# Twelve chunks untiled, unit 4 by crossbar, unit 0's v through TensorE, unit 7's decays by small transfers: a re-planned attention and FFN kernel

## The chip, the cores and the metric

The kernel runs on one core of a Trainium2 chip. A core has TensorE (PE, matrix products into PSUM), VectorE (DVE), ScalarE (ACT), GpSimd (POOL) and SyncE (SP), which share the on-chip memory SBUF and sixteen DMA engines. In this kernel SP issues the transfers of the hardware queue (loads, stores, and transpositions through the DMA crossbar); POOL issues the weights on the software queue, which turn from float32 into bf16 on the way. The metric is the device time of one execution in microseconds (us). Before the change it is 196.26 us, the median of three runs (196.06 to 196.44).

## What is computed

```python
f = 1.0 / (1.0 + np.exp(-f_logit))                  # (4, 8, 768, 48)
state = np.zeros((B, H, D, D))
for t in range(S):
    state = f[:, :, t, :, None] * state + np.einsum('bhd,bhe->bhde', k[:, :, t], v[:, :, t])
    y[:, :, t] = np.einsum('bhd,bhde->bhe', q[:, :, t], state)
x = y.transpose(0, 2, 1, 3).reshape(B * S, H * D)   # 3072 tokens, 384 wide
gate = np.maximum(x @ w_gate, 0.0)                  # 1536 wide
out = (gate * (x @ w_val)) @ w_out
```

A gated linear attention (4 batches, 8 heads, 768 tokens, head size 48) feeds an FFN with two input matrices and one output matrix.

## The kernel before

**Units and chunks.** A chunk is 128 tokens of one batch, 24 in all. A unit is two chunks that follow each other, numbered y = 0 and 1; unit u holds chunks w = 2u and 2u + 1, and the twelve units go through the batches in turn (`seq`), so that unit u + 4 takes up the state that unit u left. Four chunks, two units, are a group of 512 tokens for the FFN; group g needs units 2g and 2g + 1. A load brings two neighbouring tokens to each partition, so even and odd tokens are apart (index i).

**A unit** (`unit`, L603). ScalarE takes exp and log of the forget logits (L620, L622). TensorE forms cumulative sums (`cum`, L629 and L630; where `even` is DVE, VectorE derives one of the two, L633), ScalarE their exponentials (L641, L644, L651; `qps` says whether q's stay in PSUM), and VectorE or POOL multiplies them into q and k, the "hats". Then there are two ways. In the units of `pe_hats` a hat is made whole (L663), and TensorE transposes it (L703), after which a copy brings it to SBUF as `qkT` (`tk`, `tq`). In the other units the hats are made in halves of 64 rows (L669) and SP sends them through the crossbar (L725). `q_lined` lists units whose q lies in order of tokens. v is put in order by copies of 64 rows: four into `vpad`, and in units of `pe_hats` two more into `vrest`, each on an engine that a dictionary names (`v00` to `v11`, `r0`, `r1`). Scores are matmuls on 48 rows, two at a time in different rows of TensorE (L739); a mask follows, on VectorE (L752) or by a copy on ScalarE and a product on POOL (L747, L749; `m00` to `m11`). `total` (L759, L763) with an exp (L768) gives the decays, `state` (L777 untiled, L787 in two row tiles for `pe_hats`) the new part of the state, which L589, L594 and L597 put together on VectorE and POOL.

**The output of a chunk** (`out_of`, L799) has two forms. Chunks in `pe_x` take `intra` (L819): 28 matmuls, 16 where there is no state yet, in four column tiles of 32, whose result is transposed already and is copied to `xT`. The others take `natural` (L826, L830): twelve untiled matmuls, a copy to `xn`, and a crossbar transposition by SP into `xT` (L848). Their rows come out with even and odd tokens apart, so their output is stored in two halves.

**The FFN.** `ffn_hidden` (L854) is for each of twelve j three gate and three val matmuls of 512 columns (L866), ScalarE's relu (L872) and VectorE's product (L878). In group 0 the first five j are done in halves of 256 columns, two chunks at a time. `ffn_out` (L883) is twelve matmuls of 384 columns for each chunk (L894), in steps of three.

**The order.** Every instruction is added to a plan with a duration, a latency, a priority (small is early) and what it reads and writes. `Plan.schedule` then simulates the engines and the two DMA rings and picks, again and again, the instruction that can start first; among equals, the one of smaller priority. Each engine executes its own list in that order, waiting on semaphores. FFN pieces form one chain with a priority of P + 60. `pace` names an FFN piece that has to start before a unit's cumulative sum may. `slack` adds 1 us to the planned end of a unit's transfers if they start after EASY = 34. While the first 24 us are planned to leave TensorE idle, it is given filler matmuls (L950, L958). `first` writes the order of the first loads; "wg2@f2" is slice 2 of w_gate, issued when f of unit 2 has landed. A load waits for the fifth load ahead of it.

```python
key = (at, op.prio, op.idx)
if u in pe_hats or (n == "q" and u not in q_lined):
if w in pe_x:
```

Of the kernel before, what the change touches and what calls it, by code (L numbers as in the profile page):

```python
# [13 lines left out]
class Op:  # L14
# [4 lines left out]
                 "after", "follows", "flow", "goal", "floor", "ring", "descs", "deps0", "crosses", "slack", "tiles", "port", "early", "held")  # L19

    def __init__(self, eng, emit, reads, writes, occ, lat, prio, opens=(), after=(), follows=()):
# [14 lines left out]
        self.port = False  # L36
        self.held = False
# [14 lines left out]
class Rings:  # L52
# [27 lines left out]
    def worked(self, t):  # L80
        work = t - self.now
        for p in self.PAUSES[self.passed:]:
            if p >= t:
                break
            work -= max(0.0, min(t, p + self.PAUSE) - max(self.now, p))
        return work

    def later(self, work):
        t = self.now
        for p in self.PAUSES[self.passed:]:  # L90
            if t + work <= p:
                break
            work -= max(0.0, p - t)
            t = max(t, p + self.PAUSE)
        return t + work

    def next(self):
        found = None
        for r, q in self.queue.items():
            if q:  # L100
                t = self.later(self.left[r] / self.speed(r))
# [6 lines left out]
    def step(self, t, ring):  # L108
        speeds = {r: self.speed(r) for r in self.RATE}
        for r, q in self.queue.items():  # L110
            if q:
                self.left[r] -= self.worked(t) * speeds[r]
# [17 lines left out]
class Plan:  # L130
# [3 lines left out]
    EASY = 26.0  # L134
    hot_until = 0.0
# [43 lines left out]

    def schedule(self, banks):  # L180
# [9 lines left out]
        free = dict(self.free0)  # L190
        waiting = {e: [] for e in self.ENGINES}
# [34 lines left out]
        while True:  # L226
            pick = None
            for e in self.ENGINES:
                for op in waiting[e]:
# [13 lines left out]
                    key = (at, op.prio, op.idx)  # L243
# [14 lines left out]
            (at, _, _), op, slot = pick  # L258
            e = op.eng
            waiting[e].remove(op)  # L260
# [92 lines left out]
def bass_hgrn2_outer__then__ffn_reglu_kernel(  # L353
# [23 lines left out]
    wsteps = 4  # L377
    WJ = NJ // wsteps
    first = 'f0 v0 f1 k0 q0 f2 wg2@f2 wg0@f2 wv0@f0 wv1@v0 k1 wg1@k1 q1 wv2@q1 v1 k2@wv0 q2 wg3@q2 wv3@v0 wo1@f0 wo0@f1 wo2@f0 wo3@f0 f3@wg2 q3@wv0 k3@wg1 v2@wo1 v3@wv0'.split()
    seq = [(0, 0), (1, 0), (2, 0), (3, 0), (0, 1), (1, 1), (2, 1), (3, 1), (0, 2), (1, 2), (2, 2), (3, 2)]  # L380
    pe_hats = {0, 1, 2, 3, 4, 5}
    pe_x = {0, 1, 2, 3, 4, 5, 6, 7, 9, 10, 11, 12, 13, 21, 22, 23}
    q_lined = {0, 1, 4, 7, 8, 9, 10}
# [20 lines left out]
    vrest = [sb(f"vrest{i}", [128, HD], BF16) for i in range(NV // 2)]  # L404
    st = [[sb(f"st{b}_{i}", [128, SW], BF16) for i in range(2)] for b in range(B)]
# [12 lines left out]
    gT = [sb(f"gT{i}", [128, NJ, GT], BF16) for i in range(NG)]  # L418
    NR = 4
# [14 lines left out]
    pl = Plan({'bc': 3, 'tp': 2, 's': 4, 'y': 1, 'kv': 2, 'f': 4})  # L434
    pl.EASY = 34
# [61 lines left out]
    for name, t, cols, value, prio in (("halves", halves, 4, 1.0, -27), ("other", other, 64, 1.0, -26), ("away", away, 16, 16.0, -26)):  # L497
# [8 lines left out]
        ["ident"], ["ident"], occ=0.25, prio=-28)  # L506
    fill("DVE", "zeros", zeros[:], 0.0, 256, -30)
# [29 lines left out]
    def load(n, u, after=()):  # L537
# [4 lines left out]
        behind = list(after) + (sent[-5:][:1] if len(sent) >= 5 else [])  # L542
        op = chain("load", "SP", lambda: sy.dma_start(dst, src), [], [f"{n}{u % NL}"], occ=0.65, lat=1.3, prio=u * 20 - 40, after=behind)
        dma(op, f"{n}{u % NL}", 1.27, 1, 1024)
# [5 lines left out]
    def load_w(nm, s, after):  # L550
        if nm == "wo":
            src = bass.AP(tensor=w_out.tensor, offset=s * WJ * 128 * DM,
                          ap=[[DM, 128], [128 * DM, WJ], [1, DM]])
            dst = wo[:, s * WJ:(s + 1) * WJ, :]
        else:
            src = bass.AP(tensor=wsrc[nm].tensor, offset=s * WJ * 128,
                          ap=[[DFF, 128], [128 * DFF, NK], [1, WJ * 128]])
            dst = (wg if nm == "wg" else wv)[:, :, s * WJ * 128:(s + 1) * WJ * 128]
        op = chain("load_w", "POOL", lambda: gp.dma_start(dst, src), [], [f"{nm}{s}"], occ=0.79, lat=2.3,
                   prio=-10 if s == 0 else 30, after=after)  # L560
        dma(op, f"{nm}{s}", 6.0 / wsteps, ring="sw")
        return op

    done = {}

    def begin(items):
        for item in items:
            item, _, behind = item.partition("@")
            need = [done[x] for x in behind.split("&")] if behind else []
# [3 lines left out]
    t4 = lambda t: t[:, 0:HD].rearrange("p (n j e) -> p n j e", n=NP, j=2)  # L573
    QROW = NQ * 4 * NP * C

# [475 lines left out]
```

## Time and profile before

| | us |
|---|---|
| median of three runs | 196.26 |
| the profiled execution, its own time | 196.28 |
| its span, first to last instruction | 194.5 |
| TensorE busy | 187.0 |
| VectorE busy | 131.1 |
| ScalarE busy | 123.2 |
| POOL busy | 75.2 |
| first FFN matmul starts | 20.38 |
| last FFN matmul group starts (60 of L894) | 184.18 |

By stretches of ten us, busy time:

| stretch | TensorE | VectorE | ScalarE | POOL |
|---|---|---|---|---|
| 0 to 10 | 8.63 | 5.10 | 6.94 | 3.81 |
| 10 to 20 | 8.73 | 8.99 | 8.22 | 7.21 |
| 20 to 30 | 9.53 | 7.65 | 7.33 | 5.29 |
| 60 to 70 | 9.79 | 9.08 | 9.87 | 6.45 |
| 110 to 120 | 9.35 | 7.96 | 5.01 | 5.61 |
| 160 to 170 | 10.00 | 4.48 | 2.98 | 0.00 |

In the profile, L866 is line 866 of the kernel. A row of the order in time gives start, duration, engine, line, operation, what is written and read, the tiling, the shape and how many instructions of that kind follow each other; in brackets stands the idle time ahead of it and what ended it. Matmuls are pipelined: a row's duration holds the time that the last one takes to leave the array, so the next row starts before it ends. What a piece costs is read from the starts. "PEld" is the loading of weights into the array, SPq and POOLq the queues that issue transfers.

### The profile page before, as it was taken

Reading aid. Unit: us, or ns where it says so; the run is one execution under the profiler, and the core shown is the slowest. Engines: PE = TensorE matmul, PEld = TensorE weight load, DVE = VectorE, ACT = ScalarE, POOL = GpSimd, SP = SyncE. Lnnn points to the kernel's source line nnn. Section 1 sums busy time; section 2 is a strip of 40 time slices with the busy share of each in tenths; the row PEclk is TensorE's granted clock in tenths of the full one; section 3 lists DMA queues with packets and bytes.
Section 4 is the critical chain, followed back from the end, with each engine's and each line's share of the span. In section 5 each row is a group of like instructions: output and inputs, shape, how many; then the busy total and the mean of one; then the engine's idle time right before and its main releaser. Section 6 shows DMA issues by size and latency. Waiting matters only on the chain.

```text
span 194.5 us, 4615 instructions
## 1 busy us (share of the span) xinstructions
PE 187.0 (96%) x1827; PEld 104.7 (54%) x1850; DVE 131.1 (67%) x247; ACT 123.2 (63%) x239; POOL 75.2 (39%) x105
## 2 busy tenths in 40 slices
PE   7988999999999999999999999999999999999995
PEld 2355684655655545555555555555455455544564
DVE  4589975875799896996699976337988533442310
ACT  4997769888398999959597455336364633344312
POOL 5286458058518624096468852000056210000000
PEclk9999999999999999999999999999999999999999
DMA  6999999995999899899965472201344301111113
GB/s 163 325 290 201 255 264 193 213 275 154 318 282 286 214 323 304 185 226 219 305 186 116 80 148 66 66 16 40 93 96 89 82 18 28 44 40 40 40 43 119
DMA packets 74469, 31.36 MB, mean 161 GB/s; under 512 B 66640, under 2 KB 74448, under 8 KB 74448
## 3 DMA queue, kind: packets, MB, share of 16 engines
q1 hardware_dynamic: 69648, 27.53, 55.5%
q0 software_dynamic: 4800, 3.54, 12.0%
q8 instruction: 14, 0.23, 0.5%
q14 instruction: 7, 0.06, 0.1%
HBM read 25.95 MB, written 4.72 MB: 158 GB/s over the span
## 4 chain that ended last, share of the span: by engine, by line
PE 73%; ACT 11%; DVE 10%; issue 3%; DMA 2%; POOL 0%; SPq 0%; DVEq 0%
PE ps L866 37%; PE ps L894 21%; PE ps L819 3%; PE ps L958 3%; DVE ptm L752 2%; PE ps L703 2%; ACT relu L872 2%; PE ps L739 2%; DVE hats L669 2%; DVE gT L878 2%; DMA qkT<-hats 2%; ACT ptm L747 1%; ACT expo L644 1%; ACT f_in L620 1%; ACT ps L651 1%
## 5 line engine op out<-in xcount | busy, mean ns | idle before, releaser
L878 DVE TENSOR_TENSOR gT<-relu,ps 128x512 bf16<-128x512 bf16 (+1 forms) x77 | 49.4, 649 | 33.4 <-PE ps L866 30.2
L872 ACT ACTIVATE relu<-ps 128x512 bf16<-128x512 f32 (+1 forms) x77 | 43.7, 570 | 31.5 <-PE ps L866 31.0
L866 PE MATMUL ps<-xT,wv 128*128 128x512 bf16 (+1 forms) x225 | 58.0, 365 | 0.8 <-issue 0.5
L866 PE MATMUL ps<-xT,wg 128*128 128x512 bf16 (+1 forms) x216 | 56.2, 364 | 1.1 <-DVE st L589 0.2
L894 PE MATMUL ps<-wo,gT 128*128 128x384 bf16 (+2 forms) x300 | 52.0, 320 | 0.0
L894 PEld LDWEIGHTS ps<-wo,gT 128*128 128x128 bf16 x300 | 27.8, 98 | 18.6
L866 PEld LDWEIGHTS ps<-xT,wv 128*128 128x128 bf16 x231 | 21.4, 98 | 22.3 <-DVE ptm L752 0.4
L866 PEld LDWEIGHTS ps<-xT,wg 128*128 128x128 bf16 x231 | 21.4, 98 | 19.3 <-DVE st L589 0.4
L749 POOL TENSOR_TENSOR ptm<-ptm,seen 128x512 bf16<-128x512 bf16 x20 | 22.8, 1154 | 23.1 <-ACT ptm L747 23.1
L597 POOL TENSOR_TENSOR st<-ssum,dec 128x384 bf16<-128x384 f32 x16 | 13.3, 830 | 42.7 <-DVE ssum L594 39.5
L752 DVE TENSOR_TENSOR ptm<-ps,seen 128x512 bf16<-128x512 f32 x28 | 17.8, 683 | 2.4 <-PE ps L739 2.3
L474 ACT ACTIVATE osb<-ps 128x384 f32<-128x384 f32 (+2 forms) x10 | 4.6, 459 | 16.5 <-PE ps L894 16.5
L475 DVE COPY osb<-ps 128x384 f32<-128x384 f32 x15 | 8.3, 554 | 8.3 <-PE ps L894 8.2
L669 DVE TENSOR_TENSOR hats<-k_in,ps 64x384 bf16<-64x384 f32 x24 | 13.2, 550 | 0.6 <-ACT ps L651 0.3
L747 ACT ACTIVATE ptm<-ps 128x512 bf16<-128x512 f32 x20 | 11.1, 598 | 4.1 <-PE ps L739 4.0
L669 POOL TENSOR_TENSOR hats<-q_in,expo 64x384 bf16<-64x384 f32 x12 | 11.9, 995 | 1.3 <-ACT expo L644 0.6
L651 ACT ACTIVATE ps<-ps 128x384 f32<-128x384 f32 x24 | 10.8, 484 | 0.0
L620 ACT ACTIVATE f_in<-f_in 128x768 f32<-128x768 f32 x12 | 10.1, 840 | 1.1 <-DMA f_in<-in_f_logit_dram 1.0
L474 ACT ACTIVATE xT<-ps 128x384 bf16<-128x384 f32 x11 | 6.6, 601 | 6.2 <-PE ps L819 5.9
L958 PE MATMUL ps<-zeros 128*128 128x512 bf16 x31 | 9.7, 461 | 0.6 <-DVE hats L663 0.6
L622 ACT ACTIVATE bneg<-f_in 128x768 bf16<-128x768 f32 x12 | 10.1, 841 | 0.1
L474 ACT ACTIVATE vpad<-v_in 64x384 bf16<-64x384 f32 x19 | 9.9, 520 | 0.3
(83 smaller groups left out, 200.8 us busy)
## 6 DMA issues: line engine op xcount, KB each, us to landing
f_in<-in_f_logit_dram SPq DMA_DIRECT2D x12, 384.0 KB, 5.0
v_in<-in_v_dram SPq DMA_DIRECT2D x12, 384.0 KB, 5.0
k_in<-in_k_dram SPq DMA_DIRECT2D x12, 384.0 KB, 5.0
q_in<-in_q_dram SPq DMA_DIRECT2D x12, 384.0 KB, 5.1
out_dram<-osb SPq DMA_DIRECT2D x15, 192.0 KB, 2.6
out_dram<-osb SPq DMA_DIRECT2D x16, 96.0 KB, 2.2
wg<-in_moe_w_gate_dram POOLq DMA_DIRECT2D x4, 288.0 KB, 5.7
wv<-in_moe_w_val_dram POOLq DMA_DIRECT2D x4, 288.0 KB, 6.8
```

The lines of the kernel that those rows point to most:

```text
L474: return sc.activation(out, src, AF.Copy)
L597: add(e, lambda: engine[e].tensor_tensor(t4(s_new), t4(tmp), rate, ALU.mult), [key] + dk, [f"S{b}_{y}"], prio=P + 2, **(dict(occ=0.79, lat ...
L651: add("ACT", lambda i=i, ex=ex: sc.activation(bc[i].ap[:, 0:HD] if in_place else ex[:, 1, :], bc[i].ap[:, 0:HD], AF.Exp, scale=1.0), [bc[i ...
L669: op = add(e, lambda i=i, n=n, x=x, e=e, y=y, lo=lo, exps=exps: engine[e].tensor_tensor(hats[64 * i:64 * i + 64, hi, y, x, :, 0:D], by_i[n ...
L747: add("ACT", lambda pt=pt, s=sj[j]: sc.activation(pt, s.ap[:, :].rearrange("p (n t) -> p n t", n=NP), AF.Copy), [sj[j]], [f"raw{mis[y]}_{j ...
L749: add("POOL", lambda pt=pt, mask=mask: gp.tensor_tensor(pt, pt, mask, ALU.mult), [f"raw{mis[y]}_{j}", "seen"], [f"raw{mis[y]}_{j}", f"ptm{ ...
L752: add("DVE", lambda pt=pt, mask=mask, s=sj[j]: ve.tensor_tensor(pt, s.ap[:, :].rearrange("p (n t) -> p n t", n=NP), mask, ALU.mult), [sj[j ...
L866: mm = te.matmul(bank.ap[:, 0:n], wt[:, kt, j * 128:(j + 1) * 128], xT[xi][:, kt, n0:n1], start=(kt == 0), stop=(kt == NK - 1))
L872: add("ACT", lambda: sc.activation(relu[ri][:, 0:n], gate.ap[:, 0:n], AF.Relu), [gate], [f"relu{ri}"], prio=P, **act_t(n))
L878: add("DVE", lambda: ve.tensor_tensor(gT[gi][:, j, n0:n1], relu[ri][:, 0:n], val.ap[:, 0:n], ALU.mult), [val, f"relu{ri}"], [f"gT{gi}_{j}_ ...
L894: mm = te.matmul(bank.ap[:, 0:cut[1] - cut[0]], gT[gi][:, j, r * C:(r + 1) * C], wo[:, j, cut[0]:cut[1]], start=(j == 0), stop=(j == NJ - 1))
L958: return te.matmul(bank.ap[:, 0:WARM], zeros[:, 0:128], zeros[:, 0:WARM], start=True, stop=True, skip_group_check=True)
```

## The change

- **Tiling in the plan.** Pieces of TensorE get a mode: "rows" (scores, state in `pe_hats`, the new v), "columns" (`intra`), else "whole". A change of mode is planned with 0.095 us ahead (TURN), and among pieces that can start at the same moment, and after a tiled one, those of the same mode come first, other tiled ones second.
- **Chunks.** `pe_x` loses chunks 5, 9, 12 and 13, so that twelve of 24 go through `natural` and the crossbar.
- **Units.** `pe_hats` loses unit 4, which goes through the crossbar. `q_lined` gains 2, 5 and 6 (2 and 5 are in `pe_hats`, so it tells for unit 6 only).
- **v of unit 0** (`vpe`). One copy brings v to bf16 (`vrow`); two pairs of matmuls with `ident` and `swap` put its rows in place in PSUM, and two copies on ScalarE go to `vpad`. The state of unit 0 reads `vrow`. POOL makes `swap` by two copies.
- **Decays of unit 7** (`td`). In place of `total` and its exp, SP writes two rows of the exponentials to a buffer in device memory and reads them back by four transfers of 192 single elements each.
- **Plan settings.** The weights of group 0 come in the order of `first` below; a load waits for the sixth ahead of it, not the fifth. EASY goes from 34 to 55, slack from 1 to 0.5, the FFN's priority from P + 60 to P + 20; pauses that are assumed for the transfer rings apply to the hardware ring alone. Group 0 does six j in halves, not five. `pace` is new, and three instructions have their priority shifted. Some durations in the plan change.
- **Waits that only order** (`late`, `yy`): unit 2's state comes behind its qkT, unit 1's first chunk behind the masks of both chunks.
- **Engines.** The dictionary of each unit is new, so masks, copies and products change engines. Unit 0: both masks of its first chunk on VectorE, x of the first chunk on ScalarE and of the second on VectorE. Unit 1: both copies of qkT on ScalarE. Several output copies go from VectorE to ScalarE. `even` by TensorE: units 0, 1, 2, 6, 7 for 0, 1, 3, 5, 6.

Lists that don't act here (empty sets for weights by another way) are left out. `UNITS` stands for the dictionary, which the kernel's text writes out at each use.

```diff
+    TURN = 0.095
+    def stay(self, mode, new):
+        if mode == "whole" or new == "whole":
+            return 2
+        return 0 if new == mode else 1 if self.STAYS else 2
...
-                    key = (at, op.prio, op.idx)
+                    key = (at, self.stay(mode, op.mode) if e == "PE" else 2, op.prio, op.idx)
...
+            if e == "PE":
+                if op.mode != mode:
+                    at = max(free[e] + self.TURN, at)
+                mode = op.mode
...
-    first = 'f0 v0 f1 k0 q0 f2 wg2@f2 wg0@f2 wv0@f0 wv1@v0 k1 wg1@k1 q1 wv2@q1 v1 k2@wv0 q2 wg3@q2 wv3@v0 wo1@f0 wo0@f1 wo2@f0 wo3@f0 f3@wg2 q3@wv0 k3@wg1 v2@wo1 v3@wv0'.split()
+    first = 'f0 v0 f1 q0 k0 wg0@k0 wv0@k0 wv1@k0 wg1@k0 v1 wg2@v1 wv2@f1 k1 q1 f2 k2@wg2 v2 q2 wg3@q2 wv3@k0 k3@wv0 f3 wo1@f3 wo0@q1 q3 wo3@q3 wo2@q3 v3@wv2'.split()
...
-    pe_hats = {0, 1, 2, 3, 4, 5}
-    pe_x = {0, 1, 2, 3, 4, 5, 6, 7, 9, 10, 11, 12, 13, 21, 22, 23}
-    q_lined = {0, 1, 4, 7, 8, 9, 10}
+    pe_hats = {0, 1, 2, 3, 5}
+    pe_x = {0, 1, 2, 3, 4, 6, 7, 10, 11, 21, 22, 23}
+    q_lined = {0, 1, 2, 4, 5, 6, 7, 8, 9, 10}
...
-    pl.EASY = 34
+    pl.EASY = 55
+    pl.STAYS = True
...
-        behind = list(after) + (sent[-5:][:1] if len(sent) >= 5 else [])
+        behind = list(after) + (sent[-6:][:1] if len(sent) >= 6 else [])
...
+            if vpe:
+                lo, vps, e1 = 64 * y, Bank("vp"), on.get(f"vc{y}", "ACT")
+                def spread(lo=lo, y=y, vps=vps):
+                    for i in range(2):
+                        mm = te.matmul(vps.ap[:, 0:HD], (ident if i == y else swap)[lo:lo + 64, :], vr[lo:lo + 64, i, :],
+                                       start=(i == 0), stop=(i == 1))
+                    return mm
...
+        if on.get("td") and not qb and 2 * u >= NA:
+            at = 2 * u * HD
+            op = add("SP", lambda at=at: sy.dma_start(
+                bass.AP(tensor=rates, offset=at, ap=[[HD, ny], [1, HD]]),
+                bass.AP(tensor=expo, offset=63 * EROW + (ei * 2 + 1) * 2 * HD, ap=[[64 * EROW, ny], [1, HD]])),
+                [f"expq{ei}_1"], [f"rates{u}"], occ=0.36, lat=0.9, prio=P + 2.4)
+            dma(op, f"rates{u % 4}", 0.15, 1, 2)
+            for y in range(ny):
+                for j in range(2):
+                    row = bass.AP(tensor=rates, offset=at + y * HD + j * D, ap=[[1, D], [2 * D, NP]])
+                    col = bass.AP(tensor=dec_all, offset=64 * j * DROW + (a0 + y) * NP * 2 + j, ap=[[DROW, D], [2, NP]])
+                    op = add("SP", lambda row=row, col=col: sy.dma_start(col, row, allow_slow_non_contiguous=True), [f"rates{u}"],
+                             [f"dec{a0 + y}" + "_1" * j], occ=0.5, lat=0.9, prio=P + 2.5)
...
-                op.slack = 1 if op.flow is not None else 0
-        for r0, r1, js in {0: [(0, 2, range(0, 5)), (2, 4, range(0, 5)), (0, 4, range(5, 12))]}.get(g, [(0, GC, range(NJ))]):
+                op.slack = 0.5 if op.flow is not None else 0
+        for r0, r1, js in {0: [(0, 2, range(0, 6)), (2, 4, range(0, 6)), (0, 4, range(6, 12))]}.get(g, [(0, GC, range(NJ))]):
...
-    pace = {4: 0, 6: 22, 9: 29, 8: 32, 10: 46, 5: 6, 7: 18, 11: 44}
+    pace = {9: 6, 10: 26, 6: 12, 5: 12, 3: 7, 7: 18, 8: 30}
...
+        op.prio += {'SP v1 2': 40, 'ACT vrest0_1 0': 18, 'PE f 143': 38}.get(f"{what} {met[what]}", 0)
```

161 lines of the change are left out of this document (109 added, 52 removed).

## The prediction

> **What bounds the kernel now.** I read the page first. Its first part says that TensorE is busy nearly throughout, its second where it is not: in the first eighth and in the last slice. The DMA engines are full in the first half.
>
> ```profile
> PE 187.0 (96%) x1827; PEld 104.7 (54%) x1850; DVE 131.1 (67%) x247; ACT 123.2 (63%) x239; POOL 75.2 (39%) x105
> PE   7988999999999999999999999999999999999995
> DMA  6999999995999899899965472201344301111113
> ```
>
> A busy share includes filler work and the turns between tilings, so I went on to the order in time. At the start TensorE runs fillers (L958) between pieces of units 0 and 1; the FFN (L866) begins at 20.38.
>
> ```profile
> 7.20 2.53 PE L958 MATMUL ps<-zeros 128*128 128x512 bf16 x11
> 17.12 0.41 PE L819 MATMUL ps<-ptm,vpad 128*32 128x128 bf16 x16
> 20.38 0.50 PE L866 MATMUL ps<-xT,wg 128*128 128x256 bf16 x3 [0.22 <-DVE st L589]
> 35.37 0.81 PE L866 MATMUL ps<-xT,wg 128*128 128x512 bf16 x3
> 41.46 5.54 PE L894 MATMUL ps<-wo,gT 128*128 128x384 bf16 x33
> ```
>
> From about 29 on TensorE sets the end. What a piece of attention costs there is the time from the end of the FFN piece ahead of it to the start of the next one. A gate or val piece (three matmuls) takes 0.648 us: 71.31 to 71.96 in its own rows. The first four rows show a tiled chunk (L819) between such pieces, the next four an untiled one (L826, L830), the last two a transposition on TensorE (L703).
>
> ```profile
> 71.96 0.81 PE L866 MATMUL ps<-xT,wg 128*128 128x512 bf16 x3
> 72.70 0.35 PE L819 MATMUL ps<-qkT,st 128*32 128x128 bf16 x12
> 72.88 0.40 PE L819 MATMUL ps<-ptm,vpad 128*32 128x128 bf16 x16
> 73.20 0.82 PE L866 MATMUL ps<-xT,wv 128*128 128x512 bf16 x3
> 60.23 0.81 PE L866 MATMUL ps<-xT,wv 128*128 128x512 bf16 x3
> 60.88 0.33 PE L826 MATMUL ps<-st,qkT 128*128 128x96 bf16 x4
> 61.04 0.36 PE L830 MATMUL ps<-vpad,ptm 128*128 128x48 bf16 x8
> 61.25 0.81 PE L866 MATMUL ps<-xT,wg 128*128 128x512 bf16 x3
> 66.74 0.61 PE L703 MATMUL ps<-ident,hats 128*128 128x128 bf16 x8
> 67.19 0.81 PE L866 MATMUL ps<-xT,wg 128*128 128x512 bf16 x3
> ```
>
> The tiled chunk costs 73.20 - 71.96 - 0.648 = 0.59, of which 0.09 passes before it begins; the untiled one 0.37, with nothing ahead; eight transposes 0.45. Last, the waits of TensorE and the DMA issues: a crossbar transfer that landed late held TensorE in one place only.
>
> ```profile
> 116.94 0.62 PE L739 MATMUL ps<-qkT 48*128 48x128 bf16 x16 [0.42 <-DMA qkT<-hats]
> 26.69 0.80 POOL L559 DMA_DIRECT2D wg<-in_moe_w_gate_dram  x1 [3.20 <-DMA q_in<-in_q_dram]
> ```
>
> **The change part by part.** The sum is against the profiled execution: 194.5 of span and 1.78 around it, 196.28; the median shown is 196.26, so it stands for both.
>
> Untiled x. Chunks 5, 9, 12, 13 leave the tiled form: 4 x (0.59 - 0.37) = -0.89. Each adds one crossbar transfer (SP issue 1.25, landing 2.3 to 3.8) behind a plain copy that replaces the tiled one (0.49 or 0.55 against about 0.6), and stores in two halves (0.47 of SP each). Those lie in SP's queue beside TensorE; their lateness is priced below.
>
> Unit 4 by crossbar. Two banks of transposes go: 2 x 0.45 = -0.90. Its state leaves the row-tiled form. That took 0.11 of entry and 0.51 from 65.64 on; eight untiled matmuls take 0.34 (81.09 to 81.43): -0.28. VectorE loses two copies of 0.68 and gains four more half hats of 0.55, 0.8 more, beside TensorE (it is busy 67%). SP gains two issues of 1.28 with landings of 3.0 to 5.8. Together -1.18.
>
> Unit 7's decays. The nine small matmuls of `total` take 0.20 (79.73 to 79.95): -0.20; ScalarE is spared one exp of 0.19. In exchange come five transfers, the four reads behind the landing of the write, so SP stands still for a landing (1.6 at least by the stores) with loads and transposes of later units behind it. The cover: unit 7's cumulative sums run at 78.91 and its state at 94.07, so 15 us are there; I take nothing.
>
> Unit 0's v. Two pairs of 384-column matmuls at 0.16 each, 0.66, fall in the stretch that holds eleven fillers: nothing (+0.66 if the cover is gone). The reordering copy (0.88 at most, the 128x768 rows of ScalarE's exp being 0.84) replaces six small ones on three engines.
>
> Turns. A fresh tiled chunk (16 matmuls) takes 0.34, a full one (28) 0.50: 0.0133 a matmul, which leaves 0.13 that doesn't scale; with the 0.09 of entry a turn and back costs 0.22. The Trainium skill, TensorEngine Tiling (Array Packing), section Tiling Modes, says that changing the tiling mode drains TensorE, and gives no price; by that rule a neighbour in another tiled mode would save no drain, only one in the same mode. The sum by it would lack the next term, and be 0.4 higher. The planner now prefers, among pieces ready at once, one of the same tiling, and then another tiled one. What it will find ready no row shows: between 0 and 17 entries (12 chunks, 5 states) at 0.10. I take four, -0.4, near the lower end, since the rows show most tiled pieces single.
>
> Start. The masks of unit 0's first chunk go to VectorE both; before, POOL's ended at 16.62, VectorE's first two at about 15.4. The second chunk's copy leaves ScalarE, where it waited behind a 1.02 copy of qkT. So both could be 0.9 to 1.2 earlier. ScalarE gets more: two copies of v (0.49) and the first x (0.60) against one rest copy, a mask copy's equal and the second x, +0.45 in unit 0, and one qkT copy of 1.02 in unit 1. It sat idle 1.9 between 4.3 and 20.4, so 1.47 fits but only just. The bounds are -2.2 (the 1.2, and k's exps ahead of unit 1's by one more us) and +1.5 (all of ScalarE's addition). I take -0.5.
>
> Order of loads. Weights wait for k of unit 0, fifth in SP's queue, at about 9.1 (issue 4.30 and q's shortest landing 4.8), not for f of unit 2 at 10.63; they begin with slice 0. But slice 3 of w_gate waits for q of unit 2, now behind v too, and w_out has v2 and q3 ahead of it. Its need was at 35.37 and w_out's at 41.46. I put q2's landing at about 28 against 26.69; with a landing of 5.5 to 8.2 slice 3 comes at 33.5 to 36, needed at some 34.9. Wait: 0 to 3.4 (the slowest q, 6.8, and the slowest wg, 8.2); I take +0.3, as the medians just fit.
>
> Late crossbars. One of 20 held TensorE, 0.42. There will be 26: the same share is 0.55, part of which the smaller loads may spare; I take +0.3. Ends 0 and 13 (26 x 0.5, the slack taken away).
>
> The sixth gate and val in halves costs TensorE 12 x 0.11 against 6 x 0.216, nothing; q of unit 6 in four halves costs VectorE 1.1, the additional output copies ScalarE some 2 us around 41 to 55, where it is busy three quarters: nothing. POOL's two copies for `swap` lie in its wait for v (2.26).
>
> Sum: -0.89 - 1.18 - 0.20 - 0.40 - 0.50 + 0.30 + 0.30 = -2.57, and 196.28 - 2.57 = 193.7.
>
> **The rivals.** First, slower: the plan's slack. TensorE takes its pieces in the order written, so a transfer later than planned holds it at that piece, whatever lies behind. The plan added 1 us to each transfer started after 34; now 0.5 after 55. For it: DMA is full till 100, and landings spread by 2.6 (3.2 to 5.8) and 1.4 (2.4 to 3.8). Against it: only one of 20 waited. If nine of 26 wait 0.5, that is 4.5 where 0.3 is in the sum: 197.9. It decides above six waits of 0.5.
>
> Second, no change: the start gives everything back. ScalarE's 1.47 and unit 2's 0.59 on the path, and -0.5 gone, makes 193.7 + 0.5 + 2.06 = 196.3; slice 3 of w_gate at its latest does about the same (193.7 - 0.3 + 3.4 = 196.8 at the far end). For it: ScalarE fills 8.2 of 10 us there. Against it: its idle 1.9.
>
> Third, faster still: the start gives 2.2, ten turns are saved, and no weight is late: -0.89 - 1.18 - 0.20 - 1.0 - 2.2 + 0.3, 191.1.
>
> Fourth, unit 7's decays come late. The hardware queue's 69648 packets took 55.5% of 16 engines' 194.5 us, 0.025 us each; 192 single elements are 4.8 us if one engine takes them, 19 for four. With 15 covered and a write of 2.2 ahead, 6 remain at worst; taking half, 196.7. The Trainium skill, DMA: Bandwidth & Descriptors, section Rules for kernel authors, says that a strided last dimension lowers to one descriptor per element, which is what this rival rests on; no row here has such a transfer. Spread over 16 engines it is 0.3 each, and hidden.
>
> **How the numbers follow.** Forecast 0.57 (its own range 191.9 to 195.6: start and turns at their better values, or turns at 0 and the start at +1.0); slack 0.21; start given back 0.10; faster still 0.08; decays 0.04. A measurement of this kernel tells 0.2% from no change, 0.4 us. Faster: 0.57 + 0.08 = 0.65; same 0.10; slower 0.21 + 0.04 = 0.25. The range reaches down to 191.1, and up to 198.2, which leaves about half of the slack's chance outside.
>
> **What would show it.** In the changed kernel's rows: 12 crossbar transfers of xT and 14 of qkT; 80 transposes on TensorE; eleven totals; the first FFN piece at about 19.9; untiled chunks with no gap ahead; some tiled pieces next to each other. Wrong: waits of TensorE on DMA in more than six places, or the FFN's start after 21. Most open are the start, where several engines are full at once, and what the new order finds ready.

## The result, and the profile after

The change makes the kernel slower: 197.12 us (median of 17 runs, 196.24 to 197.93) against 196.26 for the kernel before (17 runs beside them, 195.89 to 196.90). The ratio is 1.0046, with a 95% interval of 1.0032 to 1.0061. The forecast was 193.7, faster, so its side was wrong; the time lies inside the stated range of 191.1 to 198.2. Executions over 1.5% longer than the fastest of their kernel (none here) are left out of all ratios below, while medians and ranges hold them.

One thing has to be known before the trace is read: the profiled execution of the changed kernel took 196.24, the fastest of its 17, with a span of 194.5, which is also that of the kernel before. So this trace shows a good execution. What the median has on top of it, 0.88 us, it cannot show.

The first parts of the page of the changed kernel: busy time by engine, then TensorE and DMA in forty slices.

```profile
PE 185.0 (95%) x1739; PEld 103.9 (53%) x1762; DVE 127.0 (65%) x237; ACT 130.6 (67%) x256; POOL 74.0 (38%) x103
PE   7899888999999999999999999999999999999995
DMA  5999999999999989998899993178211100111113
```

TensorE is busy 2.0 us less than before in the same span, so it stands still for longer. The row of slices says where: the fifth to seventh slice, 19.5 to 34, have an 8 where the kernel before had a 9. From 34 on there is no other digit than 9 up to the last slice, as before.

The order in time on TensorE through group 0, rows after the FFN's start (start, duration, engine, line, operation, operands, tiling, shape; in brackets the idle time ahead and what ended it):

```profile
18.55 0.50 PE L952 MATMUL ps<-xT,wg 128*128 128x256 bf16 x3 [0.29 <-DVE xT L505]
19.96 0.62 PE L806 MATMUL ps<-qkT 48*128 48x128 bf16 x16
21.21 0.38 PE L1050 MATMUL ps<-zeros 128*128 128x512 bf16 x1 [0.63 <-ACT relu L958]
...
27.80 0.50 PE L952 MATMUL ps<-xT,wv 128*128 128x256 bf16 x3 [0.70 <-DVE hats L712]
...
29.46 0.62 PE L770 MATMUL ps<-ident,hats 128*128 128x128 bf16 x8 [0.50 <-DVE hats L712]
30.72 0.62 PE L770 MATMUL ps<-ident,hats 128*128 128x128 bf16 x8 [0.64 <-DVE hats L712]
...
44.82 2.12 PE L980 MATMUL ps<-wo,gT 128*128 128x384 bf16 x12
47.19 0.66 PE L980 MATMUL ps<-wo,gT 128*128 128x384 bf16 x3 [0.24 <-DMA wo<-in_moe_w_out_dram]
```

The FFN starts at 18.55 (20.38 before), as the forecast wanted and more. But then come four waits of 0.5 to 0.7 and one of 0.24, where the kernel before had in this stretch none above 0.2 but the 0.22 of its first row. Group 0's pace can be read from four marks:

| start of | before | after | after less before |
|---|---|---|---|
| first FFN piece | 20.38 | 18.55 | -1.83 |
| first 512-column FFN piece | 29.09 | 34.36 | +5.27 |
| first w_out matmul | 41.46 | 44.82 | +3.36 |
| group 1's first gate | 52.93 | 55.32 | +2.39 |
| last w_out block (60 matmuls) | 184.18 | 184.15 | -0.03 |

(The second mark overstates: twelve j in halves stand before it now, against ten.) Two things follow from the last two rows. From group 1 on, the changed kernel needs 184.15 - 55.32 = 128.83 where the kernel before needed 131.25: it wins 2.42 there. And group 0, from the FFN's first piece to group 1's, takes 36.77 in place of 32.55: it loses 4.22.

Of the 4.22, about 0.9 is work that only changed places: sixteen scores of unit 1 (0.55), two cumulative sums (0.33) and a set of totals (0.22) now stand behind the FFN's start, while one chunk, untiled now, costs 0.22 less. The waits of the fence in its rows from 21.21 on are another 2.9, the one filler matmul of 0.22 that is put into the first of them included.

What holds them is in the chain of waits of the changed kernel (start, duration, what; each row is released by the one above it or follows it on its engine; pieces under 0.05 are left out):

```profile
14.68 7.66 DMA wg<-in_moe_w_gate_dram
22.35 0.37 SPq L578
22.76 5.50 DMA v_in<-in_v_dram
28.29 0.55 DVE vpad L502
28.85 0.55 DVE hats L712
...
30.72 0.64 PE ps L770 x8
31.38 1.02 ACT qkT L504
...
34.40 2.26 POOL ptm L817 x2
36.66 0.75 POOL wo L606
37.41 9.73 DMA wo<-in_moe_w_out_dram
47.15 0.05 issue
47.19 0.66 PE ps L980 x3
```

From slice 2 of w_gate to w_out it is one chain; only TensorE's wait at 21.21, for ScalarE's relu, is not part of it. Slice 2 of w_gate lands at 22.35; SP, whose load of k for unit 2 waits for it, stands until then, with v and q of unit 2 queued behind; k lands at about 27.2 and v at 28.26. VectorE has to wait for k, here in its own order in time, and makes the hats late (the three waits of TensorE between 27 and 31):

```profile
27.19 0.55 DVE L712 TENSOR_TENSOR hats<-k_in,ps 128x384 bf16<-128x384 f32 x1 [1.18 <-DMA k_in<-in_k_dram]
```

The masks on POOL come late in turn, and the last two slices of w_out, which POOL issues behind those masks, leave only at 36.66 and 37.41. In the kernel before, all four slices were issued from 28.25 to 31.3, and TensorE needed the first at 41.46. The SP queue's own waits show the first step: in the kernel before, its longest waits for a transfer were these two,

```profile
SPq L543 <- DMA wo<-in_moe_w_out_dram: 9.3, 1, 9.3
SPq L543 <- DMA wv<-in_moe_w_val_dram: 9.0, 1, 9.0
```

and in the changed kernel there is one (total, times, longest):

```profile
SPq L578 <- DMA wg<-in_moe_w_gate_dram: 12.1, 1, 12.1
```

So one wait grew and one is gone. The one that is gone, "v2@wo1", had kept SP off the DMA engines while w_out came in. Now v of unit 3, f and k of unit 4 are issued at 29.44, 30.77 and 32.36, ahead of and beside w_out.

### The profile page after: what moved, and what is told of

Same layout as the page of the kernel before. It is cut to its first block, busy times and chain, and to the rows that moved or that the text cites. A ratio compares the mean times of both kernels' runs of the same rounds, so it can differ in the third digit from the quotient of the medians.

```text
span 194.5 us, 4468 instructions
## 1 busy us (share of the span) xinstructions
PE 185.0 (95%) x1739; PEld 103.9 (53%) x1762; DVE 127.0 (65%) x237; ACT 130.6 (67%) x256; POOL 74.0 (38%) x103
## 4 chain that ended last, share of the span: by engine, by line
PE 69%; DMA 14%; ACT 6%; POOL 4%; issue 2%; DVE 2%; SPq 2%
PE ps L952 36%; PE ps L980 23%; DMA wo<-in_moe_w_out_dram 5%; DMA wg<-in_moe_w_gate_dram 4%; DMA v_in<-in_v_dram 3%; DMA k_in<-in_k_dram 2%; SPq L578 2%; PE ps L806 2%; ACT relu L958 2%; PE ps L904 1%; POOL ptm L817 1%; PE ps L860 1%; PE ps L915 1%; PE ps L770 1%; PE ps L911 1%
## 5 line engine op out<-in xcount | busy, mean ns | idle before, releaser
L980 PE MATMUL ps<-wo,gT 128*128 128x384 bf16 (+2 forms) x300 | 50.6, 320 | 0.2 <-DMA wo<-in_moe_w_out_dram 0.2
L980 PEld LDWEIGHTS ps<-wo,gT 128*128 128x128 bf16 x300 | 28.4, 98 | 19.9 <-DMA wo<-in_moe_w_out_dram 0.6
L817 POOL TENSOR_TENSOR ptm<-ptm,seen 128x512 bf16<-128x512 bf16 x23 | 26.2, 1154 | 21.5 <-ACT ptm L815 21.5
L504 ACT ACTIVATE osb<-ps 128x384 f32<-128x384 f32 (+2 forms) x17 | 7.9, 468 | 19.7 <-PE ps L980 19.7
L820 DVE TENSOR_TENSOR ptm<-ps,seen 128x512 bf16<-128x512 f32 x25 | 16.2, 685 | 6.2 <-PE ps L806 6.0
L718 DVE TENSOR_TENSOR hats<-k_in,ps 64x384 bf16<-64x384 f32 x28 | 15.4, 551 | 1.6 <-ACT ps L700 1.0
L505 POOL CAST vpad<-v_in 64x384 bf16<-64x384 f32 x13 | 6.5, 500 | 21.9 <-DMA v_in<-in_v_dram 20.7
L504 ACT ACTIVATE vpad<-v_in 64x384 bf16<-64x384 f32 x23 | 12.0, 521 | 1.9 <-DMA v_in<-in_v_dram 1.5
L815 ACT ACTIVATE ptm<-ps 128x512 bf16<-128x512 f32 x23 | 12.6, 599 | 0.9 <-PE ps L806 0.9
L643 DVE TENSOR_TENSOR ssum<-ps,st 128x384 f32<-128x384 f32 x16 | 8.8, 551 | 1.4 <-PE ps L860 0.9
```

What stands on the lines that cost most here:

```text
L504: return sc.activation(out, src, AF.Copy)
L718: op = add(e, lambda i=i, n=n, x=x, e=e, y=y, lo=lo, exps=exps: engine[e].tensor_tensor(hats[64 * i:64 * i + 64, hi, y, x, :, 0:D], by_i[n ...
L815: add("ACT", lambda pt=pt, s=sj[j]: sc.activation(pt, s.ap[:, :].rearrange("p (n t) -> p n t", n=NP), AF.Copy), [sj[j]], [f"raw{mis[y]}_{j ...
L817: add("POOL", lambda pt=pt, mask=mask: gp.tensor_tensor(pt, pt, mask, ALU.mult), [f"raw{mis[y]}_{j}", "seen"], [f"raw{mis[y]}_{j}", f"ptm{ ...
L820: add("DVE", lambda pt=pt, mask=mask, s=sj[j]: ve.tensor_tensor(pt, s.ap[:, :].rearrange("p (n t) -> p n t", n=NP), mask, ALU.mult), [sj[j ...
L980: mm = te.matmul(bank.ap[:, 0:cut[1] - cut[0]], gT[gi][:, j, r * C:(r + 1) * C], wo[:, j, cut[0]:cut[1]], start=(j == 0), stop=(j == NJ - 1))
```

## The experiments

The edits are made on the finished plan, right behind `order = pl.schedule(...)`, so that no other instruction changes its place; the last two instead emit four chunks in the other form at the same place. Ratios are to the kernel before, run on the same chip.

**The changed kernel once more, for its spread.** No edit.

> The changed kernel as it is, once more, for a second profile. The profiled execution at hand took 196.24, the median of its runs is 197.12. Theory of the loads: whatever the execution, TensorE waits some 2.0 us in group 0 between 26.9 and 31 (0.86, 0.50 and 0.64 in the profile at hand), because k, v and q of unit 2 land late; a slower execution shows the same waits longer. Theory of the slack: a slower execution shows group 0 unchanged, and new waits on transfers after 55. Time expected 196.9 to 197.4.

Measured: 197.27 (196.30 to 199.61), ratio 1.0045 [1.0025, 1.0064]: the result stands. Beside it the kernel before kept to 195.70 to 196.68. The execution that was profiled here was a long one, 199.55, and it explains nothing of the 0.46%, which holds without it. It does show what lateness can cost. The waits for the hats are no longer in it than in the first profile (1.00 and 0.64), and after 55 no transfer holds TensorE; what grew is the wait for w_out, which neither theory had named. Order in time on TensorE, and the page's row of the granted clock:

```profile
44.34 2.12 PE L980 MATMUL ps<-wo,gT 128*128 128x384 bf16 x12
48.95 0.66 PE L980 MATMUL ps<-wo,gT 128*128 128x384 bf16 x3 [2.49 <-DMA wo<-in_moe_w_out_dram]
...
50.33 2.10 PE L980 MATMUL ps<-wo,gT 128*128 128x384 bf16 x6
```

```profile
PEclk9999999999699999999999999999999999999999
```

The last slice of w_out landed 12.0 after its issue; TensorE stood 2.49, and behind that the clock was granted at 0.6 in the mean of a slice of 4.9 us: six matmuls took 2.10 which take 1.15 otherwise. In shorter windows the granted clock is 1.0 up to 50.0 and 0.50 from 50.5 to 53.5, so it fell about 1.5 us after TensorE had gone on at 48.95. The mean granted clock of this execution is 0.991. Three of the twelve had that value (199.39 to 199.61), one of the 17 of the result (197.75), and none of the 118 executions of the kernel before that ran beside the experiments.

**k of unit 2 earlier.** Its load waits for slice 0 of w_val, as in the kernel before, not for slice 2 of w_gate.

```diff
+    k2 = next(o for o in pl.ops if o.eng == "SP" and o.writes == ["k2"])
+    k2.deps[done["wv0"]] = k2.deps.pop(done["wg2"])
```

> Same order on every engine; the load of k for unit 2 waits for slice 0 of w_val, not for slice 2 of w_gate, so SP goes on at about 17.5 in place of 22.35, and v and q of unit 2 with it. Theory of the loads: VectorE's wait for k2 at 26 to 27.2 goes, TensorE's three waits of together 2.0 us with it, less up to 0.7 that the weight slices now sharing the rings come later: 195.1 to 196.0. Theory of ScalarE: TensorE's first wait (20.5 to 21.4) is what counts and stays, the rest is slack that fills again: within 0.4 of the changed kernel. Theory of the slack: no change, 197.1.

Measured: 196.56 (195.42 to 197.96), 1.0021 [0.9998, 1.0045]. The profiled execution starts group 1 at 54.70 (55.32), but it still has a wait of 1.03 for the hats at 29.42, and its wait for w_out grew from 0.24 to 0.93: group 0 came earlier and w_out did not. By the ratios about half a us is given back (1.0021 against 1.0045), with intervals that overlap.

**The first relu ahead of unit 2's exp on ScalarE,** alone and with the edit above ("both").

```diff
+    a = order["ACT"]
+    i = next(n for n, o in enumerate(a) if o.writes == ["f2"])
...
+    a[i], a[i + 1] = a[i + 1], a[i]
...
```

> Same order but for two neighbours on ScalarE: the first relu of the FFN goes ahead of unit 2's exp (0.84), behind which it waits from 19.8 to 20.56 while TensorE stands from 20.5 to 21.43 with one filler. Theory of ScalarE: up to 0.75 is won and kept, 196.4. Theory of the loads: what is won there is lost again at 26.9, where TensorE waits for unit 2's k in any case: 197.1, no change.

> The two edits together. Theory of the loads and of ScalarE together: the first edit's gain and now also the second's 0.75, since nothing waits at 26.9 any more: 194.4 to 195.6, faster than the kernel before the change (196.26). If the gain is that of k2 early alone, the relu's place was covered.

Measured: the relu alone 198.26 (six runs, 196.81 to 199.66), 1.0108 [1.0061, 1.0156]; both 196.05 (195.31 to 196.33), 0.9996 [0.9983, 1.0008]. The relu's edit does take away the wait at 20.5 (0.63 and a filler become 0.16), but the waits behind it stay, and w_out holds TensorE for 1.11: by itself it did not help. That it does harm is not shown: three of the six (199.21 to 199.66) had a granted clock of 0.991, and the other three, 196.81 to 197.31, lie among the changed kernel's at full clock on this chip (196.30 to 197.87). Both together are level with the kernel before. In their profile w_out costs 1.31, and its landings take 9.2 to 10.8.

**When the late slices of w_out are issued.** First, slices 2 and 3 change places on POOL, so that the one needed first goes first ("wo_swap"). Second, both are issued ahead of the two masks ("wo_hoist"), and third the same on top of "both" ("all3").

```diff
+    p = order["POOL"]
+    i = next(n for n, o in enumerate(p) if o.writes == ["wo3"])
+    assert p[i + 1].writes == ["wo2"]
+    p[i], p[i + 1] = p[i + 1], p[i]
...
```

```diff
+    i = next(n for n, o in enumerate(p) if o.writes == ["wo0"])
+    masks, late = p[i + 1:i + 3], p[i + 3:i + 5]
...
+    p[i + 1:i + 5] = [late[1], late[0]] + masks
...
```

> The changed kernel with the last two issues of w_out on POOL in the other order, slice 2 ahead of slice 3, all else in its place. Theory of w_out: in every profile of this kernel's family TensorE waits at the third of the four steps of group 0's output (0.24 to 2.49), which needs slice 2, the last to be issued and to land; with slice 2 one place ahead that wait goes, slice 3 is needed half a us later and so waits less. Expected 196.4 to 196.8, and runs closer together than 196.24 to 199.6. Theory that only unit 2's late k counts: no change, 197.2.

> The changed kernel with slices 2 and 3 of w_out issued ahead of the two masks on POOL that hold them back by 2.3 us, and in that order. Theory of w_out: they land 2 to 3 us sooner, no wait at the output; the masks come 1.6 later, which a chunk's output, 2 us after them, may feel by up to 1. Expected 196.2 to 196.6. Theory that only unit 2's late k counts: 197.2.

> k of unit 2 released early, the relu ahead of unit 2's exp, and the slices of w_out ahead of the masks. The first two together gave 196.05 with a wait of 1.31 left for w_out. Theory of w_out: that wait goes, 194.7 to 195.4. If w_out still lands at about 46.7, since the rings are full whatever the order of issue, it stays at 196.0.

Measured: "wo_swap" 196.27, 1.0003 [0.9981, 1.0024]; "wo_hoist" 196.90, 1.0026 [1.0010, 1.0042]; "all3" 196.25, 1.0002 [0.9972, 1.0033]. The swap takes the wait for w_out out of the profile and wins some 0.8 by the ratios. The earlier issue takes that wait away too, but the slices then land after 8.5 to 14.1, and the masks, issued later, hold TensorE instead (0.62 and, with "both", 0.90 <-POOL ptm at 36). Issuing w_out earlier, beside the other transfers, bought little here.

**What runs beside w_out.** On top of "both", f of unit 4, with k of unit 4 behind it in SP's queue, waits until slice 1 of w_out has landed; this restores the quiet that "v2@wo1" had given.

```diff
+    f4 = [o for o in pl.ops if o.eng == "SP" and o.writes == ["f0"]][1]
+    f4.deps[done["wo1"]], f4.start = "raw", done["wo1"].start + 0.01
```

> The first two edits, and the load of f for unit 4 (with it k of unit 4 behind it in SP's queue) waits until slice 1 of w_out has landed, in place of running beside w_out. Theory of contention: w_out lands 8 to 10.8 after its issue because v3, f4 and k4 share the rings with it; without two of them slice 2 lands about two loads' time, 2.4, sooner and the wait of 1.31 goes: 194.8 to 195.5. Theory of issue order: w_out's landing is set by its own four slices, the wait stays, and f4 late adds to it: 196.0 to 197.

Measured: 194.24 (four runs, 194.20 to 194.59), 0.9897 [0.9885, 0.9910]: faster than either kernel. In its profile SP issues nothing between 29.2 and 39.4 (the same columns as in the order on TensorE):

```profile
28.00 1.22 SPq L578 DMA_DIRECT2D v_in<-in_v_dram  x1
39.44 0.37 SPq L578 DMA_DIRECT2D f_in<-in_f_logit_dram  x1
```

and w_out lands sooner than in "both" (9.2/10.0/10.8):

```profile
DMA to landing us min/median/max: 7.4/8.4/9.3
```

TensorE has no wait for w_out left and one for the hats, 0.64 at 29.12. Group 1 starts at 53.29 and the last block at 182.17, 128.88 later, as in the changed kernel (128.83): all that was won lies in group 0.

With the swap of slices added, without ("all_swap") and with the held load ("best"):

> k of unit 2 released early, the relu ahead of unit 2's exp, and slice 2 of w_out issued ahead of slice 3 (masks left in place). The first two gave 196.05 with a wait of 1.31 for w_out; the swap alone took that wait away and 1.0 off the median. Theory that group 0's waits are all that the change lost: 194.7 to 195.3, faster than before. Theory that later crossbar transfers then hold TensorE (as 1.35 at 93 in the profile of the run with w_out ahead of the masks): 195.6 to 196.2, and the profile shows a wait of TensorE on a transfer between 60 and 120.

> All of these: k2 early, relu first, slice 2 of w_out ahead of slice 3, f4 held behind slice 1. If each wait is its own, no wait of TensorE above 0.3 is left before 60: 194.6 to 195.2. If the transfers of units 5 to 9 come late instead (f4 and k4 held), as in the kernel before at 116.94, 195.5 to 196.3.

Measured: "all_swap" 195.56, 0.9963 [0.9940, 0.9986]; "best" 194.84 (194.20 to 197.33), 0.9923 [0.9896, 0.9949]. The first lies just under the range of the second theory, but that theory's sign is absent: in its profile (194.76) TensorE waits on no transfer between 60 and 120. The swap adds nothing to the held load: there is no wait left for it to take away.

**The three edits apart.** "hold" is the held load alone, "k2_hold" the held load and k of unit 2 earlier, without the relu's edit; the full version ran again beside them.

> The kernel after, but the loads of f and k for unit 4 (k stands behind f in SP's queue) wait until slice 1 of w_out has landed. k, v and q of unit 2 stay late and the first relu stays behind unit 2's exp. Theory (the loss is mostly w_out landing late beside later units' loads, plus the lower granted clock that follows the wait): w_out lands within some 9.5 us of its issue, TensorE has no wait on it, and the time is 194.8 to 195.8, below before. Rival (the loss is k, v and q of unit 2 behind slice 2 of w_gate): with those waits left in, the time stays at 196.5 to 197.2.

> As the run before, and k of unit 2 waits for slice 0 of w_val, not for slice 2 of w_gate; the first relu stays behind unit 2's exp. Theory (w_out's landing carries most, k's load about 0.7 as it did alone, the relu little): 194.2 to 195.0, within 0.6 of the version that also moved the relu (194.24). Rival (the relu's place at the FFN's start carries much of what that version won): 195.5 or more, as the loads' share would then be about half.

> The version with k of unit 2 earlier, the first relu ahead of unit 2's exp, and f of unit 4 held until slice 1 of w_out has landed, once more. If its time is that of the order of loads and no chance of one chip: 194.0 to 194.8, below both kernels. If the late transfers return: a spread up to 196 or more, as in the kernel after.

Measured: "hold" 196.16, 0.9999 [0.9979, 1.0018]; "k2_hold" 194.92 (194.40 to 199.24), 0.9933 [0.9912, 0.9953]; the full version 195.05 (194.21 to 196.94), 0.9948 [0.9923, 0.9973]. The held load alone landed between the two expectations: it wins about 0.9 against the changed kernel (whose ratio was 1.0046 and 1.0045), and its profile has no wait for w_out, but the waits for the hats are all there (0.98, 0.46 and 0.64). So neither cause carries it alone. Earlier k alone won 0.5, not clear of the noise; on top of the held load it wins 1.3 (0.9933 against 0.9999, on one chip), and the two together 1.1% of the time, 2.2 us. The relu's place makes no difference that these runs can tell. The gain against the kernel before stands on a second chip, with a smaller size: the spread of the first profile did return (group 1 at 56.00 in the profiled run, which took 196.94, after an FFN start of 19.81 and a wait of 0.92 for w_val). What makes the start vary like that was not tried.

The order in time on TensorE in "k2_hold", its one wait between 22 and 60:

```profile
29.52 0.62 PE L770 MATMUL ps<-ident,hats 128*128 128x128 bf16 x8 [0.90 <-DVE hats L712]
```

**The suspect put into the kernel before.** v of unit 2 no longer waits for slice 1 of w_out. Nothing else of the change is there.

```diff
+    v2 = next(o for o in pl.ops if o.eng == "SP" and o.writes == ["v2"])
+    v2.deps.pop(done["wo1"])
```

> The kernel before, with one wait taken away: v of unit 2 no longer waits until slice 1 of w_out has landed, so v of units 2 and 3 and f and k of unit 4 are issued from about 26 on, beside w_out's transfers. Theory (loads issued beside w_out make its slices land late): slices of w_out land 9 to 12 us after their issue where they took 7.4 to 9.6, TensorE waits for the last of them, and the time is 197.0 to 199.0. Rival (w_out's lateness in the kernel after comes from its later issue alone): no wait on w_out, and 196.0 to 196.5.

Measured: 197.99 (six runs, 197.10 to 198.94), 1.0087 [1.0057, 1.0117]: slower by 1.7, more than the whole change. POOL issues w_out at the same moment as before (28.38 against 28.25), SP the loads beside it:

```profile
26.43 2.47 SPq L543 DMA_DIRECT2D v_in<-in_v_dram  x2
29.00 2.13 SPq L543 DMA_DIRECT2D f_in<-in_f_logit_dram  x1
31.23 7.12 SPq L543 DMA_DIRECT2D k_in<-in_k_dram  x1
```

and w_out lands late (7.4/8.4/9.6 in the kernel before):

```profile
DMA to landing us min/median/max: 9.6/11.7/13.8
```

So loads on the hardware queue slow w_out's transfers by about 3 us, and the issue of a load stretches too (7.12, where the same queue's load issues took 0.37 to 3.32 between 16 and 48 in the kernel before). The Trainium skill, DMA: Bandwidth & Descriptors, section Queues, rings and completion order, says that each DMA engine takes turns between its queues, a packet at a time; these landings agree with that, 11.7 shared against 8.4 alone.

The expected wait on w_out, however, is hardly in this profile. The first slice is issued 13.1 us ahead of its need (28.38 to 41.52), and TensorE's weight loads waited 0.4, its matmuls not. The profiled execution (197.16) lost 0.2 up to group 1 (53.13 against 52.93), and 0.66 at the one crossbar transfer that already bound the kernel before. The chain of waits there (pieces under 0.05 left out), which has three masks on VectorE where that of the kernel before has two:

```profile
111.50 1.90 DVE ptm L752 x3
113.41 0.05 issue
113.46 0.94 SPq L917
114.40 0.05 issue
114.45 3.31 DMA qkT<-hats
117.76 0.05 issue
117.81 0.64 PE ps L739 x16
```

In the kernel before the transfer began at 113.61. What the other 0.8 of the median is, no trace here shows. So this run shows that without the wait w_out lands later and the time is 1.7 longer; that the one brings the other is not shown.

**Untiled chunks alone, in the kernel before.** Chunks 5, 9, 12 and 13 take the untiled matmuls, while the rest of their way stays as it was; the reordering and the crossbar transfer that this form needs are left out. A second edit, not shown, lets `natural` read q of these chunks as it lies.

```diff
-            chain("intra", "PE", intra, need, [bank], ...)
+            chain("intra", "PE", natural if w in (5, 9, 12, 13) else intra, need, [bank], ...)
```

> The kernel before the change, same order, with the matmuls of chunks 5, 9, 12 and 13 in the untiled form. The copy and the way to x stay those of the tiled form, no crossbar transfer is added, and for chunks 12 and 13 q is read in another order of tokens; so those chunks' results are left wrong and this measures TensorE's part of the change alone. The prediction's first term says -0.89: 195.4. If an untiled piece between FFN pieces costs TensorE as much as a tiled one once the engines behind it set the pace, no change: 196.2.

Measured: 196.30, 0.9991 [0.9977, 1.0005]: no difference in the time. The trace says why. The 97th w_out matmul starts at 106.40 where it started at 107.29: the full 0.89 of the forecast's term. Then the chain of waits of this kernel goes through SP and the crossbar:

```profile
111.60 0.47 SPq L917
112.07 0.05 issue
112.12 4.61 DMA qkT<-hats
116.77 0.62 PE ps L739 x16
```

TensorE waits 1.14 there (0.42 in the kernel before), so 0.72 is given back: the transfer starts 1.49 earlier but takes 4.61 in place of 3.28. The last block starts at 184.02, 0.16 earlier than before.

**The same chunks tiled again, on top of "both".** The reverse edit; as there, the copy and the crossbar transfer stay those of the other form.

```diff
-            chain("intra", "PE", natural, need, [bank], ...)
+            chain("intra", "PE", intra if w in (5, 9, 12, 13) else natural, need, [bank], ...)
```

> The first two edits, order unchanged, and the matmuls of chunks 5, 9, 12 and 13 tiled again (their results are then wrong, as copy and crossbar stay those of the untiled form). The kernel with the two edits took 196.05. If TensorE's work sets the time from group 1 on, 4 x 0.22 = 0.89 more: 196.9. If transfers set it, as they did where the untiled form was put into the kernel before (won 0.89 by 106, lost 0.72 of it to one crossbar transfer at 116), less than half: 196.1 to 196.4.

Measured: 196.57 (195.87 to 199.98), 1.0014 [0.9996, 1.0031], against 0.9996 [0.9983, 1.0008] for "both" on another chip: 0.35 slower, with intervals that overlap. From group 1 to the last block this run's trace needs 129.33, that of "both" 129.13; "both" has a wait of 0.28 at 62.40 that the other lacks. Without it, three chunks in that stretch cost 0.48 more when tiled, where 0.67 was expected. In the changed kernel, then, most of the term is there on TensorE; how much of it the time keeps, these runs don't tell.

## Why the prediction was wrong

**The sum of the later groups held.** Three of the four chunks that became untiled lie behind group 1's start (3 x 0.22 = 0.67), and so do unit 4 (1.18), unit 7 (0.20) and, as far as the sum goes, the turns (0.40): 2.45. The traces show 2.42. The rows behind it are as they were forecast. An untiled chunk of the changed kernel, order in time on TensorE:

```profile
36.76 0.81 PE L952 MATMUL ps<-xT,wv 128*128 128x512 bf16 x3
37.41 0.33 PE L911 MATMUL ps<-st,qkT 128*128 128x96 bf16 x4
37.58 0.36 PE L915 MATMUL ps<-vpad,ptm 128*128 128x48 bf16 x8
```

It begins 0.65 after the gate's start, with no gap. New tiled neighbours were found in three places behind the FFN's start: scores and state at 32.91 and 62.56, and scores and a chunk at 138.26. Four were taken; against the three stand two that the kernel before had, a state between two chunks at 49.30, and that are gone. Only the last two of the three lie behind group 1's start. At 0.10 each they are worth 0.20 there, not 0.40, and the sum is 2.25. (The chunk at 138.81 is in another mode than the scores ahead of it and begins right where they end, without the 0.09 ahead of a single one; so such a neighbour spares an entry too, which the other reading in the step "Turns" denied.) So the sum agrees with 2.42 within 0.2; that it does so term by term is not shown.

**The step "Order of loads" failed.** It took +0.3, with "the medians just fit", and bounds of 0 to 3.4. It looked at slice 3 of w_gate and at two loads ahead of w_out. It did not follow the wait that the change gave to k of unit 2: "k2@wg2" holds SP for 12.1, and v and q of the unit are queued behind it, then the hats, the masks and the issue of w_out, which are behind those. (q of the unit, which it put at about 28, landed shortly before 29.67, when POOL's issue of slice 3 went on.) And it did not ask what the removed "v2@wo1" had been good for: it saw a wait that went, and not that the wait had kept the rings free. In the profiled execution this step measures 0.70 + 0.50 + 0.64 + 0.24 = 2.08. By the ratios, the two edits that undo it ("k2_hold") are worth 2.2. The four versions that have both edits took 194.24 to 195.05. By their ratios they win 1.0 to 2.0 against the kernel before, where 2.57 had been forecast.

**The step "Start" failed by its size.** The FFN starts 1.83 earlier, at 18.55 where 19.9 was named. But 0.88 of that is work put behind the start, which the step did not count, and 0.85 is lost at once, from 20.58 to 21.43, where ScalarE's first relu of group 0 stands behind unit 2's exp. What was taken as -0.5 is about -0.1 in this trace. That ScalarE's added work "fits but only just" between 4.3 and 20.4 says nothing of the order in which it serves two others. What the relu's place is worth in the median, the runs cannot tell from nothing ("k2_hold" against the full version).

**Together,** against the profiled execution: the FFN's start -1.83, work put behind it +0.88 (the group's untiled chunk is in this), ScalarE +0.85, late loads +2.08, later groups -2.42, in sum -0.44. The marks give -1.83 + 4.22 - 2.42 = -0.03, so 0.41 of group 0 lies in gaps too small to be named. The median's 0.88 on top of the profiled execution is not explained by a trace of an ordinary execution. That the held load and the earlier k take it away together with the rest is shown by "k2_hold" (194.92). How much of it is w_out's landing in single executions is only argued, from the profile with the wait of 2.49.

**The rivals.** That the range held the time was luck: its upper end came from the first rival, late crossbars, which had the direction right by a mechanism that stayed away. The second, that the start gives everything back, came nearest: 196.3 to 196.8, by ScalarE's place or by a late weight. Its chance was 0.10, and the weight that it named, slice 3 of w_gate, held nothing in this trace; w_out and slice 2 did. The first, late crossbars, did not happen: after 55 TensorE waits nowhere on DMA, and the one larger wait is 0.29 for VectorE at 76.83. So the term "late crossbars" was 0 in place of +0.3 in this execution, and the 26 transfers fit, though their median landings grew (qkT 3.9 from 3.2, xT 3.6 from 2.4). The margin is not large: in "all3" one of them held TensorE for 1.35, at 93.03. The fourth, unit 7's decays, did not happen either: the reads land in 2.1, and POOL waits once for them, 1.0.

**The signs that were named.** Twelve and fourteen crossbar transfers came out as said. "TensorE waits on DMA in more than six places" and "the FFN's start after 21" both stayed away although the forecast was wrong: the waits showed as waits on VectorE, one step behind the late load. A test that asks only for the last releaser misses a late transfer with a copy in between.

## What to carry to other kernels

Before a wait between two loads is counted as a gain or as nothing, ask what it kept apart: taking one load's wait for a weight slice out of the kernel before cost 1.7 us and made the weight's slices land in 11.7 us in place of 8.4 (how much of the one is the other is not shown), and putting such a wait into the changed kernel won 0.9. For each wait that an edit adds to an in-order queue, follow everything queued behind it to the last engine, also through the instructions of other queues that come late in turn. Compare the ranges of the runs, not only the medians, and know which of the runs the profile is: here the wait for w_out was 0.24 in one profiled execution and 2.49 in another of the same kernel.

## What the runs showed of the hardware

- A wait can cost more than its length. In one execution (199.55) TensorE stood for 2.49 us; about 1.5 us after it had gone on, the granted clock fell to 0.50, from 50.5 to 53.5, and six matmuls took 2.10 in place of 1.15. The Trainium skill, TensorE: Matmul & The Clock Gate, section What's actually happening, says that the clock goes to half after an idle window of about 3.4 us. Half is what this trace shows too; but here the drop came behind 2.49 us of waiting, so the longer figure is not a safe margin; the waits of up to 1.35 for loads and transfers in the other profiles were followed by no such drop.
- In "before_free", four loads on the hardware queue beside four weight slices on the software queue made the slices land in a median of 11.7 us where they took 8.4, and the issue of one load took SP 7.12 us.
- A crossbar transfer that starts earlier need not land as much earlier: between the profiles of "nat_before" and the kernel before, 1.49 us of lead shrank to 0.16, as the transfer took 4.61 us in place of 3.28. What slowed it is not shown.
